# Moving the decay frame to the chunk's end, with eps in spare columns and a re-searched order, in a one-core RWKV-6 and feed-forward kernel

## The chip, the cores and the metric

One core of one Trainium2 chip. The metric is the device time of one launch in microseconds (us). The time before is the median of its launches. A launch over 1.5% above the fastest of the same kernel counts as slow, and ratios use the others, the fast ones, alone. In the profile PE is TensorE, PEld its weight loads, DVE VectorE, ACT ScalarE, POOL GpSimd, and SP the engine whose queue issues nearly all DMA.

## The reference, cut to what matters

```python
# attention: 4 batches x 8 heads, 768 steps, head size 48
for t in range(S):
    cur = einsum(u * k_t, v_t)                   # outer product per head
    y[:, :, t] = einsum(r_t, state + cur)
    state = w_t[..., None] * state + einsum(k_t, v_t)
# then, on 3072 rows of 384:
rms = sqrt(mean(x * x) + 1e-06);  xn = x / rms * rms_g
out = (silu(xn @ w_gate) * (xn @ w_val)) @ w_out  # 384 -> 1536 -> 384
```

## The kernel before

The sequence is cut into six chunks of 128 steps; each chunk has four batches. Within a chunk the recurrence is matmuls: `lw` is the logarithm of `w`, a matmul with a triangular mask sums it along the chunk, and its exponential scales r and k (`rkA`). A transposed copy (`rkT`) gives the products q, the mask cuts them, and q times v plus r times the state gives y. The state is carried from chunk to chunk. When a chunk's y is done, its rows are normalised (`xnr`), transposed (`xnt`) and go through the feed-forward part, while the next chunk's attention runs. A chunk change is the time at which PE goes over to the next chunk's log sums.

Everything is emitted in the order of one long string of steps; each engine executes its own steps in that order. `ld` is a load, `cs` the log sums, `rk` the scaling, `st` the state's matmuls, `sn` its update, `xn` the normalising, `xd` a transpose by DMA, `vc` a cast of v, `gv` a gate or value matmul, `warm` a matmul without use that keeps TensorE's clock up.

```python
def st_mm(self, m, j):                       # chunk m, batch j
    if m:                                    # old state enters PSUM by an identity matmul
        self.nc.tensor.matmul(ps, lhsT=self.ident, rhs=self.st[:, m % 2, j]..., start=True, stop=False)
    for i in range(NP):
        self.nc.tensor.matmul(ps[:, ...], lhsT=self.pair(ka, i), rhs=self.pair(v, i), ...)

def st_new(self, m, j, half):                # twice per batch: the two diagonal halves, decayed
    self.nc.vector.tensor_tensor(out=new[p, :, c], in0=ps[p, :, c], in1=wc[p, :]..., op=ALU.mult)

def x_rstd(self, m, j):
    self.nc.gpsimd.tensor_scalar(out=t[:, 0:1], ..., scalar1=1.0 / DM, scalar2=1e-6, op0=ALU.mult, op1=ALU.add)
    self.nc.gpsimd.tensor_tensor(out=t[:, 1:2], in0=t[:, 0:1], in1=self.mhalf, op=ALU.pow)

def xn_mul(self, m, j):                      # all 24 on DVE
    self.nc.vector.tensor_scalar(out=self.xnr[...], in0=self.xb[...], scalar1=self.rstd[...], op0=ALU.mult)
# ... (cut)
```

## Time and profile before

| | before |
|---|---|
| time, median (range) | 224.79 us (224.17 to 226.67), 3 launches |
| profiled span | 224.1 us |
| PE's dense start | 32.1 us |
| waits of PE after it | 9.2 us in twelve gaps |
| end of PE, then tail | 220.6 us, 3.5 us |

A busy share says little here, since PE's 91% holds warming matmuls and matmuls at half clock. What counts is where PE stands still and what released it. The lines for this are in the prediction.

### The profile page before, as it was taken

How to read it: one execution, taken by the hardware profiler on the slowest of the kernel's cores; microseconds unless marked ns; L12 is line 12 of the kernel's file. 1: busy time of each engine (PE TensorE's matmuls, PEld its weight loads, DVE VectorE, ACT ScalarE, POOL GpSimd, SP SyncE). 2: the span in 40 equal slices, each digit the busy share in tenths (PEclk: the TensorE clock that was granted, in tenths of full speed). 3: DMA queues.
4: the chain of work that ended last, by engine and by line, in shares of the span. 5: the costliest groups of instructions: out<-in, count | busy, mean ns of one | idle time of the engine just before them, and what ended most of it. 6: DMA issues, size and time to landing. Idle time of an engine off the chain costs nothing.

```text
span 224.1 us, 4873 instructions
## 1 busy us (share of the span) xinstructions
PE 204.1 (91%) x1844; PEld 125.7 (56%) x1844; DVE 162.8 (73%) x277; ACT 123.4 (55%) x221; POOL 97.6 (44%) x142
## 2 busy tenths in 40 slices
PE   7879679999959999996798999899999999999993
PEld 2345459986637856873344556346454654444561
DVE  4089897573987899993787977999996997116420
ACT  2423895784673688477534478336787354155201
POOL 2177886153368787221582258926672130000000
PEclk9999988999967999999699999999999999999999
DMA  6899999993999889968899994999839321001023
GB/s 155 169 216 234 272 341 321 310 207 78 237 196 219 168 166 155 215 137 160 195 209 143 194 222 110 213 226 195 172 76 229 63 73 35 0 35 38 1 93 117
DMA packets 133848, 36.95 MB, mean 165 GB/s; under 512 B 124481, under 2 KB 133825, under 8 KB 133825
## 3 DMA queue, kind: packets, MB, share of 16 engines
q1 hardware_dynamic: 133824, 36.65, 75.2%
q8 instruction: 14, 0.23, 0.4%
q14 instruction: 10, 0.07, 0.1%
HBM read 26.15 MB, written 4.72 MB: 138 GB/s over the span
## 4 chain that ended last, share of the span: by engine, by line
PE 53%; DVE 18%; DMA 11%; ACT 5%; issue 5%; SPq 5%; POOL 1%; DVEq 0%; ACTq 0%; POOLq 0%
PE ps L504 28%; PE ps L520 14%; DMA rkT<-rkA 6%; DVE rkA L375 4%; SPq L290 4%; PE ps L491 3%; DVE qts L403 3%; DVE st L434 3%; DVE ht L512 3%; DMA in_rk<-in_r_dram 2%; ACT junk L464 2%; DVE xb L460 2%; PE ps L400 2%; DMA in_w<-in_w_dram 2%; DMA in_rk<-in_k_dram 2%
## 5 line engine op out<-in xcount | busy, mean ns | idle before, releaser
L508 ACT ACTIVATE sg<-ps 128x512 bf16<-128x512 f32 x72 | 42.5, 595 | 45.9 <-PE ps L504 33.8
L512 DVE TENSOR_TENSOR ht<-ps,sg 128x512 bf16<-128x512 f32 x72 | 48.0, 684 | 22.8 <-ACT sg L508 15.7
L504 PE MATMUL ps<-xnt,wv 128*128 128x128 bf16 (+2 forms) x360 | 57.3, 301 | 0.5 <-DVE ht L512 0.5
L504 PE MATMUL ps<-xnt,wg 128*128 128x128 bf16 (+2 forms) x360 | 56.8, 299 | 0.6 <-DVE xnt L342 0.6
L520 PE MATMUL ps<-wo,ht 128*128 128x384 bf16 x288 | 51.5, 326 | 0.0
L504 PEld LDWEIGHTS <-wg 128*128 128x128 bf16 x360 | 29.4, 100 | 17.4 <-issue 1.7
L504 PEld LDWEIGHTS <-wv 128*128 128x128 bf16 x360 | 29.4, 101 | 16.5 <-issue 1.0
L520 PEld LDWEIGHTS <-ht 128*128 128x128 bf16 x288 | 27.6, 98 | 19.5 <-DVE ht L512 0.9
L456 POOL TENSOR_TENSOR ydr<-in_v,diag 128x384 f32<-128x384 f32 x24 | 20.6, 864 | 23.1 <-DVE diag L451 14.1
L403 DVE TENSOR_TENSOR qts<-ps,mask_lt 128x1024 bf16<-128x1024 f32 x24 | 28.8, 1216 | 1.4 <-PE ps L400 1.3
L444 POOL TENSOR_TENSOR ruk<-in_rk 128x384 f32<-128x384 f32 x24 | 24.2, 1010 | 9.9 <-DMA in_rk<-in_r_dram 4.8
L375 DVE TENSOR_TENSOR rkA<-in_rk,ps 128x768 bf16<-128x768 f32 x24 | 22.3, 947 | 4.8 <-ACT ps L372 2.8
L448 POOL TENSOR_TENSOR ruk<-ruk,u_bc 128x384 f32<-128x384 f32 x24 | 23.9, 998 | 1.6
L372 ACT ACTIVATE ps<-ps 128x768 f32<-128x768 f32 x24 | 18.8, 798 | 10.1 <-PE ps L367 9.2
L469 POOL TENSOR_SCALAR rstd<-rstd 128x1 f32<-128x1 f32 x24 | 5.2, 216 | 35.6 <-ACT junk L464 34.9
L464 ACT ACTIVATE junk<-xb 128x384 bf16<-128x384 bf16 x24 | 12.5, 520 | 13.0 <-DVE xb L460 12.9
L491 PE MATMUL ps<-mask_lt 128*128 128x512 bf16 x60 | 16.4, 415 | 1.3 <-POOL mask_lt L255 1.3
L333 ACT ACT_TABLE_LOAD x12 | 15.4, 1283 | 0.9 <-PEq L564 0.7
L434 DVE TENSOR_TENSOR st<-ps,wcr 48x192 bf16<-48x192 f32 x40 | 13.4, 352 | 1.1 <-ACT wcr L360 0.4
L470 POOL TENSOR_TENSOR rstd<-rstd,mhalf 128x1 f32<-128x1 f32 x24 | 13.3, 556 | 2.0
L451 DVE TENSOR_REDUCE diag<-ruk 128x8 f32<-128x384 f32 x24 | 12.9, 544 | 1.5 <-POOL ruk L448 1.4
L460 DVE TENSOR_TENSOR xb<-ps,ydr 128x384 bf16<-128x384 f32 x24 | 12.8, 548 | 1.3 <-PE ps L416 1.1
(62 smaller groups left out, 197.4 us busy)
## 6 DMA issues: line engine op xcount, KB each, us to landing
in_rk<-in_k_dram SPq DMA_DIRECT2D x24, 192.0 KB, 3.8
in_w<-in_w_dram SPq DMA_DIRECT2D x24, 192.0 KB, 3.9
in_rk<-in_r_dram SPq DMA_DIRECT2D x24, 192.0 KB, 3.8
in_v<-in_v_dram SPq DMA_DIRECT2D x24, 192.0 KB, 3.9
out_dram<-obr SPq DMA_DIRECT2D x24, 192.0 KB, 2.1
ht<-in_moe_w_gate_dram SPq DMA_DIRECT2D x4, 384.0 KB, 4.9
ht<-in_moe_w_val_dram SPq DMA_DIRECT2D x4, 384.0 KB, 6.1
ht<-in_moe_w_out_dram SPq DMA_DIRECT2D x4, 384.0 KB, 5.5
```

The source lines that it names most:

```text
L372: self.nc.scalar.activation(out=ps, in_=ps, func=AF.Exp)
L375: self.nc.vector.tensor_tensor(out=self.rkA[:, self.slot["rkA", m, j], :, :, 0:D], in0=self.in_rk[:, self.slot["in_rk", m], j], in1=self.b ...
L403: self.nc.vector.tensor_tensor(out=self.qts[:, self.slot["qts", m, j]].rearrange("p a q t -> p (a q) t"), in0=self.b2(("qb", m, j)).rearra ...
L434: self.nc.vector.tensor_tensor(out=new[p, :, c], in0=ps[p, :, c], in1=wc[p, :].to_broadcast([D, NP, D]), op=ALU.mult)
L444: self.nc.gpsimd.tensor_tensor(out=self.ruk[:, self.slot["ruk", m, j]], in0=rk[:, 0], in1=rk[:, 1], op=ALU.mult)
L448: self.nc.gpsimd.tensor_tensor(out=t, in0=t, in1=self.u_bc, op=ALU.mult)
L456: self.nc.gpsimd.tensor_tensor(out=self.ydr[:, self.slot["ydr", m, j]], in0=self.in_v[:, self.slot["in_v", m], j], in1=self.diag[:, m * SB ...
L491: self.nc.tensor.matmul(self.b1(("warmb",)), lhsT=self.mask_lt, rhs=bc_mid(self.mask_lt, 4), start=True, stop=True)
L504: self.nc.tensor.matmul(ps[:, a * n:(a + 1) * n], lhsT=w[:, c, f * 128:(f + 1) * 128], rhs=x[:, c], start=(a == 0 and c == 0), stop=(a == ...
L508: self.nc.scalar.activation(out=self.sg[:, self.slot["sg", m, g, i]], in_=self.b1(("gvb", m, g, i, "g")), func=AF.Silu)
L512: self.nc.vector.tensor_tensor(out=self.ht[:, self.slot["ht", m], fs[0]:fs[-1] + 1, t0:t0 + n], in0=self.b1(("gvb", m, g, i, "v")).rearran ...
L520: self.nc.tensor.matmul(ps, lhsT=self.ht[:, self.slot["ht", m], f, j * L:(j + 1) * L], rhs=self.wo[:, f, :], start=(f == 0), stop=(f == FC ...
```

## The change

It has five parts. (1) The frame of the decay moves to the chunk's end: the old state is decayed first (on POOL in 17 of 20 cases), used, and added to the new products on DVE, so the identity matmul goes. (2) The 1e-6 sits in four spare columns of `xb`, so that the sum of squares contains it and one POOL operation per row block goes. (3) Normalising and copies are spread over DVE, ACT and POOL. (4) The first chunk's feed-forward runs on groups of two batches; weights come in rows of 3 KB, and there are 36 warming matmuls instead of 60. (5) The order of all steps was searched again.

```diff
-        if m:
-            self.nc.tensor.matmul(ps, lhsT=self.ident, rhs=self.st[:, m % 2, j]..., start=True, stop=False)
-    def st_new(self, m, j, half):
-        self.nc.vector.tensor_tensor(out=new[p, :, c], in0=ps[p, :, c], in1=wc[p, :]..., op=ALU.mult)
+    def st_add(self, m, j, eng="DVE"):
+        if m:
+            self.nc.vector.tensor_tensor(out=self.sf[:, j], in0=ps, in1=self.st[:, m % 2, j], op=ALU.add)
+        else:
+            self.copy(eng, self.sf[:, j], ps)
+    def st_decay(self, m, j, eng):
+        (self.nc.vector if eng == "DVE" else self.nc.gpsimd).tensor_tensor(
+            out=self.st[:, m % 2, j]..., in0=self.sf[:, j]..., in1=self.wcr[...].to_broadcast([128, NP, 2, D]), op=ALU.mult)
-        for i, mask in ((0, self.mask_lt), (1, self.mask_nle)):
+        for i, mask in ((0, self.mask_nge), (1, self.mask_gt)):
# ... (cut)
+        for i, c in enumerate(EPS):              # EPS = four numbers, their squares / 384 sum to 1e-6
+            nc.vector.memset(self.xb[:, :, DM + i], c)
-        self.nc.gpsimd.tensor_scalar(out=t[:, 0:1], ..., scalar1=1.0 / DM, scalar2=1e-6, op0=ALU.mult, op1=ALU.add)
-    def xn_mul(self, m, j):
-        self.nc.vector.tensor_scalar(...)
+    def xn_mul(self, m, j, eng):
+        self.scale(eng, out, x, self.rstd[:, m * SB + j, 1:2])
-GROUPS = {0: ((0, 1), (1, 1), (2, 1), (3, 1)),
+GROUPS = {0: ((0, 2), (2, 2)), ...
# ... (cut: the order, and loads and casts of the weights)
```

## The prediction

> **What bounds the kernel now.** I read the page's shares first, then busy time by stage, then the gaps on TensorE (PE), then the groups.
>
> ```profile
> PE 204.1 (91%) x1844; PEld 125.7 (56%) x1844; DVE 162.8 (73%) x277; ACT 123.4 (55%) x221; POOL 97.6 (44%) x142
> PEclk9999988999967999999699999999999999999999
> DMA  6899999993999889968899994999839321001023
> ```
>
> PE is busy 91%, but that counts matmuls that only keep it warm and busy time at half clock, so the page alone doesn't settle it. The table by stage does (columns: stretch, its length, then busy time and count of PE, PEld, DVE, ACT, POOL, then granted clock, DMA share, GB/s):
>
> ```profile
> 20.00:32.00 12.00, 8.25 (x118) 5.64 (x115) 11.00 (x26) 9.70 (x23) 9.14 (x14) 1.00 0.99 267
> 32.00:49.00 17.00, 16.88 (x277) 16.81 (x277) 11.63 (x24) 12.22 (x28) 8.40 (x13) 0.90 1.05 295
> 80.00:97.00 17.00, 16.31 (x196) 12.29 (x195) 16.63 (x29) 11.39 (x20) 8.71 (x14) 1.00 0.95 178
> 97.00:110.00 13.00, 9.66 (x96) 6.22 (x95) 9.49 (x18) 9.76 (x15) 4.34 (x7) 0.90 0.71 153
> 150.00:165.00 15.00, 14.49 (x127) 8.14 (x126) 14.66 (x28) 10.56 (x18) 10.41 (x15) 1.00 0.88 180
> 181.00:200.00 19.00, 19.00 (x106) 9.32 (x105) 8.57 (x17) 8.02 (x17) 2.25 (x6) 1.00 0.14 37
> ```
>
> There are three regimes. Up to 32 us DMA is full and PE waits for inputs or runs warming matmuls. From 32 us PE carries the time, with DVE beside it at 98% where two chunks of attention overlap (80 to 97 and 150 to 165 us). From 181 us PE alone is full. So I cut the span at PE's dense start:
>
> ```profile
> 32.12 1.34 PE L504 MATMUL ps<-xnt,wg 128*128 128x128 bf16 x12 [0.60 <-DVE xnt L342]
> 64.66 0.50 PE L480 MATMUL ps<-ident,xnr 128*128 128x128 bf16 x3 [1.35 <-DVE xnr L473]
> 107.31 0.47 PE L367 MATMUL ps<-lw,mask_nle 128*128 128x384 bf16 x1 [2.96 <-DVE obr L342]
> 208.88 11.71 PE ps L520 x72
> ```
>
> The first three are from PE's timeline, with the gap before each in brackets. The last is the end of the chain of waits: 72 output matmuls in one piece to 220.6 us. Twelve bracketed gaps lie after 32.1 us (0.3, 0.8, 1.4, 0.4, 0.2, 0.5, 3.0, 0.4, 0.7, 0.6, 0.5, 0.5), 9.2 us together. Half clock after gaps costs more: in 5 us stretches the granted clock is 0.93 at 35 us, 0.52 at 65, 0.74 at 105 (half of it idle) and 0.92 at 110, so 0.35 + 2.4 + 0.7 + 0.4, plus 0.65 for the first 12 feed-forward matmuls, which took 1.34 us instead of 0.67: 4.5 us. So the span of 224.1 us is 32.1 us until the dense start, then 188.5 us to PE's end (9.2 of gaps, 4.5 of slow clock, about 174.8 of work), and 3.5 us of tail.
>
> **What the Trainium skill says.** "TensorE: Matmul & The Clock Gate", section "Wait — 56ns, not 53.3ns?", gives the warm start-to-start time as N/2.4 GHz plus about 2.5 ns. The trace agrees: 72 output matmuls of 384 columns in 11.71 us are 162.6 ns each, and 168 of 128 columns in 9.38 us (chain, at 39.6 us) are 55.8 ns. The same page, "What's actually happening", says that the clock falls to half after at least one idle window of some 3.4 us and comes back after a busy one. The clock of 0.52 after the gaps around 62 to 66 us fits. "SBUF — State Buffer", section "SBUF: two separate sides", says that POOL and some DVE operations take a shared port pair as an exclusive lock. The normalising multiply on DVE has a median of 311 ns and a longest of 1043 ns, which fits such blocking but doesn't prove it. "DMA: Bandwidth & Descriptors", "Why small descriptors are slow (HBM only)", puts a fixed cost on each packet. Here stretches of nothing but 192-byte rows moved about 215 GB/s at full DMA share, and stretches with weights in 1 KB rows up to 340.
>
> **The change, part by part.**
>
> *Identity matmul.* Sixteen matmuls of 384 columns (chunks 1 to 4, four batches) go: in the timeline such a one is followed by the next matmul after 0.17 us. 16 x 0.165 = 2.6 us less on PE, all after 32 us, so all of it counts.
>
> *State update.* Before, 40 DVE multiplies of 352 ns, 13.4 us. After, 16 DVE adds of PSUM and old state plus two copies on DVE and two on ACT. The nearest row is the addition into xb (PSUM plus SBUF, 384 columns, 548 ns): 18 x 0.55 = 9.9 us. The decay is 17 times on POOL, nearest row ydr<-in_v,diag with 864 ns: 14.7 us, and three times on DVE, 1.7 us. DVE's saving is only 13.4 - 11.6 = 1.8 us. The decay now needs this chunk's log sums, but its reader also waits for exponentials, a DMA transpose (3.2 us to landing) and the mask, so a decay of 0.9 us has slack.
>
> *Eps in spare columns.* 24 POOL operations go: 5.2 us of POOL, and some 0.2 us from each chain square, power, multiply, transpose. The square has 388 columns instead of 384: nothing.
>
> *Placement.* Of 24 normalising multiplies (458 ns) DVE keeps 13, minus 5.0 us; ACT takes 7 (about 0.5 us as its other 384-column work), POOL 4 (1.3 us, an estimate from 937 ns for 256 columns and some 0.2 us fixed). Transposed copies move from DVE (6 to 1, minus 3.4 us at 682 ns) to ACT (2 to 7, plus 5.1 us). Sums: DVE 162.8 - 1.8 - 5.0 - 3.4 and about -0.5 of small items = 152; ACT 123.4 + 3.5 + 5.1 - 2 (fewer casts, more copies) = 130; POOL 97.6 + 14.7 + 5.2 - 5.2 + 0.7 = 113. None becomes a bound over the whole; DVE is relieved by perhaps 2 us in each of its full stretches.
>
> *Chunk 0's feed-forward* goes from 288 matmuls of 128 columns to 144 of 256: 288 x 55.8 = 16.1 us against 144 x 110 = 15.8. Nothing in stream time; half the weight loads, in the stretch where PEld is 99% busy. But weights are now cut by contraction rows, so the first block needs three pieces per matrix instead of one.
>
> *Start.* Before the first block can run densely, the new order has loaded sixteen inputs of 0.197 MB, u, and seven weight pieces of 0.393 MB. At the rates above: 3.35 MB / 215 GB/s = 15.6 us, 2.75 MB / 335 GB/s = 8.2 us, plus 2.7 us to the first landing and some 1.5 us for a queue that isn't full at first: 28 us. Cast, value matmul and transposes add 1.5 to 2: dense start at about 30 us against 32.1. Gain 2 us. Warming matmuls fall from 60 to 36, which is worth nothing by itself: they fill waits.
>
> *Order.* The largest gap (3.0 us at 104) comes from DVE, which sat 3.3 us before a value cast until 105.08 us because the loads stood behind two DMA transposes in the issue queue; PE then lacked a bank. In the new order chunk 3's value loads stand before the second transpose of that group. Also fewer transposed copies and multiplies queue on DVE at 60 to 66 us. I take half of the 9.2 us of gaps as gone (4.6), and of the slow clock nearly half (2).
>
> *Sum:* 2.6 + 0.3 + 2 + 4.6 + 2 = 11.5 us at best guess; I give back 2.5 us for new waits that a searched order gets wrong on the chip. Net 9: span 215, and as the timed median is 0.7 us above the span, 216 us.
>
> **Rivals.**
> (a) *Only the matmul.* The gaps move, total unchanged: 224.8 - 2.6 - 0.3 = 222. For it: gaps come from in-order queues meeting DMA landings, which a search doesn't know exactly. Against: the largest is a named ordering fault, and the change to placement unloads the DVE where it is full.
> (b) *The start gets worse.* DMA is full until 50 us and the first block waits for six pieces instead of two. If casts or slot waits hold the issue queue, the dense start slides to 34 us or more, with warming inside: 222 to 226. For it: the new order itself keeps some warming matmuls between chunk 0's feed-forward blocks. Against: weight rows are three times longer (3 KB), and the scale column is issued early on another queue, where before it landed at 10.2 us.
> (c) *POOL becomes the new wait.* 14.7 us of decay on POOL stand before the power operation that every normalised row needs, and the shared lock lengthens DVE. Then PE waits for transposed rows: 221 to 226. For it: the 1043 ns case. Against: POOL has 10 to 15 us free in most chunks, and loses 24 small operations.
> (d) *Nearly all gaps close.* 224.8 - 2.9 - 3 - 9.2 - 4.5 = 205; I think 208 the practical limit, as some waits at chunk changes are in the data flow.
>
> **Range and chances.** The sum centres on 216; (d) bounds it below, (a) above. Eight in ten: 209 to 222. Faster by over 2% means below 220.3, which needs half of the expected saving: 0.77. Within 2%: 0.20. Slower: 0.03, since nothing adds work to PE.
>
> **What would show it.** The rows: no identity matmul, 16 DVE adds near 550 ns, decays on POOL near 0.86 us, no second POOL operation before the power. PE's timeline: dense feed-forward from about 30 us, gaps after that of 5 us or less in sum, no gap of 3 us at the change to chunk 3. The stage table: DVE below 95% where it was 98%, POOL near 113 us in all. Wrong if the dense start is later than 32 us, if PE's gaps after it still sum to 9 us, if the low-clock stretches are as many as before, or if POOL's decay or power operation is named as the releaser of long waits.

## The result, and the profile after

The changed kernel took 217.87 us (217.25 to 218.17, 4 launches) against 224.64 us (4 launches, one more than in the table above); the ratio is 0.9701, with a 95% interval of 0.9648 to 0.9754: faster. Here and below, a ratio is the mean time of one kernel's fast runs over that of the other's of the same rounds, so not quite the ratio of the medians quoted.

Three lines of the page after:

```profile
PE 194.1 (90%) x1660; PEld 119.0 (55%) x1660; DVE 151.8 (70%) x244; ACT 128.1 (59%) x232; POOL 111.4 (52%) x139
PEclk9999999999999999999699999999999999999999
DMA  6999979999999899999999798999557512221013
```

PE's busy time is 10 us less, of which 24 fewer warming matmuls are a part that buys nothing. DVE, ACT and POOL are near what the sums foretold (152, 130 and 113). The clock falls in one slice instead of several; read in shorter stretches it is at half from about 103.6 to 107 us. And the DMA row holds 7 or more, after its first slice, for 27 of the 40 slices; before, slices of 3, 6 and 4 lay among them.

The new rows, one line for each form (busy us, mean ns of one, then idle before it and its releaser):

```profile
L441 DVE TENSOR_TENSOR sf<-ps,st 128x384 f32<-128x384 f32 x16 | 8.6, 546 | 1.7 <-PE ps L435 1.7
L446 POOL TENSOR_TENSOR st<-sf,wcr 128x384 bf16<-128x384 f32 x17 | 14.0, 828 | 2.3 <-ACT wcr L363 2.2
L446 DVE TENSOR_TENSOR st<-sf,wcr 128x384 bf16<-128x384 f32 x3 | 2.2, 721 | 0.0
L477 POOL TENSOR_TENSOR rstd<-rstd,mhalf 128x1 f32<-128x1 f32 x24 | 13.5, 565 | 26.9 <-ACT junk L472 26.8
L345 POOL TENSOR_SCALAR xnr<-xb,rstd 128x384 bf16<-128x384 bf16 x4 | 5.0, 1251 | 0.3
L343 ACT ACTIVATE xnr<-xb,rstd 128x384 bf16<-128x384 bf16 x7 | 4.2, 607 | 0.8 <-POOL rstd L477 0.8
L345 DVE TENSOR_SCALAR xnr<-xb,rstd 128x384 bf16<-128x384 bf16 x13 | 6.4, 502 | 1.6 <-POOL rstd L477 1.6
```

The add on DVE takes 546 ns (0.55 us was predicted), the decay on POOL 828 (864), the multiply on POOL 1251 (1300). No second POOL operation stands before the power.

PE's timeline, the lines with its longest waits (wait and releaser in brackets), and the end of the chain of waits:

```profile
32.91 0.81 PE L511 MATMUL ps<-xnt,wg 128*128 128x256 bf16 x6 [0.52 <-DVE xnt L335]
59.49 0.40 PE L411 MATMUL ps<-rkT 48*128 48x128 bf16 x8 [0.77 <-ACT rkT L339]
92.58 0.40 PE L411 MATMUL ps<-rkT 48*128 48x128 bf16 x8 [1.14 <-DVE ht L519]
101.81 0.32 PE L370 MATMUL ps<-lw,mask_nge 128*128 128x384 bf16 x1 [1.72 <-DVE rkA L386]
131.19 0.32 PE L370 MATMUL ps<-lw,mask_nge 128*128 128x384 bf16 x1 [0.40 <-DVE rkA L386]
```
```profile
206.60 5.87 PE ps L527 x36
```

Ten gaps after the dense start sum to 5.4 us (0.77, 0.17, 0.16, 0.24, 1.14, 1.72, 0.21, 0.33, 0.40, 0.23). The dense start itself is at 32.9 us, later than before. Cut as in the prediction:

| us | before | after | difference |
|---|---|---|---|
| until the dense start | 32.1 | 32.9 | +0.8 |
| PE's waits after it | 9.2 | 5.4 | -3.8 |
| half clock | 5.8 | 1.7 | -4.1 |
| work at full clock (the rest) | 173.5 | 172.5 | -1.0 |
| tail after PE's end (212.5) | 3.5 | 3.8 | +0.3 |
| span | 224.1 | 216.3 | -7.8 |

The half clock is worked out from stretches of 0.25 us, as PE's busy time there times what the granted clock lacks to 1. The prediction's 4.5 us for before is too small. It came from stretches of 5 us, whose mean clock also counts time in which PE stands idle. Before, the clock was down from 32.2 to 35.7, 63.0 to 69.8 and 107.3 to 110.7 us, which cost 1.7, 2.6 and 1.5 us. The work after holds five warming matmuls behind the dense start, some 1.1 us.

One more view was not in the prediction's argument, though its columns were on the table: both kernels in the two stretches from 50 to 150 us (length; busy us and count of PE, PEld, DVE, ACT, POOL; granted clock, DMA share, GB/s). Before, then after:

```profile
50.00:100.00 50.00, 46.43 (x511) 34.19 (x510) 42.75 (x74) 32.51 (x60) 27.78 (x39) 0.93 0.88 175
100.00:150.00 50.00, 44.83 (x354) 23.32 (x351) 39.93 (x64) 27.36 (x44) 25.20 (x33) 0.97 0.96 182
```
```profile
50.00:100.00 50.00, 47.27 (x552) 35.53 (x551) 44.98 (x68) 38.95 (x71) 39.20 (x45) 1.00 1.03 195
100.00:150.00 50.00, 47.08 (x380) 24.74 (x379) 42.24 (x62) 28.62 (x50) 28.16 (x35) 0.97 0.99 191
```

PE is at 94%, and DMA at 99 to 103% (a share over 1 shows that this measure is no strict ceiling). In these 100 us DMA moves 193 GB/s instead of 178.5 (the means of the two stretches). So the middle of the kernel may have two near-bounds, and the new order also keeps the second one fuller.

### The profile page after: what moved, and what is told of

Read it like the earlier page. It is cut to its first block, busy times and chain, and to the rows that moved or that the text cites.

```text
span 216.3 us, 4472 instructions
## 1 busy us (share of the span) xinstructions
PE 194.1 (90%) x1660; PEld 119.0 (55%) x1660; DVE 151.8 (70%) x244; ACT 128.1 (59%) x232; POOL 111.4 (52%) x139
## 4 chain that ended last, share of the span: by engine, by line
PE 67%; SPq 8%; POOL 8%; DMA 5%; issue 4%; ACT 4%; DVE 2%; ACTq 0%; POOLq 0%; DVEq 0%
PE ps L511 37%; PE ps L527 16%; SPq L290 7%; PE ps L498 4%; PE ps L411 2%; PE ps L370 2%; DMA rkT<-rkA 2%; PE ps L427 2%; DMA xnt<-xnr 2%; POOL st L446 1%; POOL ydr L464 1%; PE ps L399 1%; POOL ruk L452 1%; DVE rkA L386 1%; PE ps L424 1%
## 5 line engine op out<-in xcount | busy, mean ns | idle before, releaser
L515 ACT ACTIVATE sg<-ps 128x512 bf16<-128x512 f32 x72 | 41.4, 596 | 37.4 <-PE ps L511 30.3
L511 PE MATMUL ps<-xnt,wg 128*128 128x256 bf16 (+1 forms) x288 | 56.3, 330 | 0.9 <-DVE xnt L335 0.5
L511 PE MATMUL ps<-xnt,wv 128*128 128x256 bf16 (+1 forms) x288 | 55.7, 329 | 0.0
L527 PE MATMUL ps<-wo,ht 128*128 128x384 bf16 x288 | 53.5, 326 | 0.0
L511 PEld LDWEIGHTS <-wv 128*128 128x128 bf16 x288 | 27.9, 99 | 18.2 <-issue 1.4
L511 PEld LDWEIGHTS <-wg 128*128 128x128 bf16 x288 | 27.1, 98 | 17.2 <-issue 1.9
L472 ACT ACTIVATE junk<-xb 128x388 bf16<-128x388 bf16 x24 | 12.6, 524 | 12.9 <-DVE xb L468 12.8
L370 PE MATMUL ps<-lw,mask_nge 128*128 128x384 bf16 x24 | 8.5, 354 | 11.3 <-ACT lw L329 8.4
L446 POOL TENSOR_TENSOR st<-sf,wcr 128x384 bf16<-128x384 f32 x17 | 14.0, 828 | 2.3 <-ACT wcr L363 2.2
L339 ACT COPY obr<-ps 128x384 f32<-128x384 f32 x14 | 6.6, 478 | 12.6 <-PE ps L527 12.4
```

What stands on the lines that cost most here:

```text
L446: (self.nc.vector if eng == "DVE" else self.nc.gpsimd).tensor_tensor(out=self.st[:, m % 2, j].rearrange("p q (a d) -> p q a d", a=2), in0= ...
L511: self.nc.tensor.matmul(ps[:, a * n:(a + 1) * n], lhsT=w[:, c, f * 128:(f + 1) * 128], rhs=x[:, c], start=(a == 0 and c == 0), stop=(a == ...
L515: self.nc.scalar.activation(out=self.sg[:, self.slot["sg", m, g, i]], in_=self.b1(("gvb", m, g, i, "g")), func=AF.Silu)
L527: self.nc.tensor.matmul(ps, lhsT=self.ht[:, self.slot["ht", m], f, j * L:(j + 1) * L], rhs=self.wo[:, f, :], start=(f == 0), stop=(f == FC ...
```

## The experiments

Twelve runs on four chips. The kernel before took 225.35, 225.74, 225.71 and 226.06 us on them. A run is read by its ratio to the kernel before of its own rounds; ratios with intervals of about 0.005 to each side tell a step of 1% apart, not one of 0.3%.

Theory: PE is the bound after its dense start, so each us taken from PE's stream or from the chains that feed it counts. Rival: in the middle PE only runs up to the next chunk change, where the feeding queues let it go; a us saved on PE is then waited away. The first batch undoes one part at a time.

### The changed kernel again, as the yardstick

> The changed kernel once more, as the level that the other runs of this batch are read against. Expected at the same ratio to the kernel before as on record, 0.970 within 0.4%.

217.37 us (216.44 to 219.69), ratio 0.9647 (0.9593 to 0.9701). The profile had PE's dense start at 32.63 us and its gap at the change to chunk 3 at 101.28 us, of 1.79 us.

### The identity matmul back

```diff
+        if m:   # result overwritten by the next matmul: same values, no new wait
+            self.nc.tensor.matmul(ps, lhsT=self.ident, rhs=v.rearrange("p h d -> p (h d)"), start=True, stop=True)
```

> The changed kernel with sixteen identity matmuls of 384 columns put back on TensorE, ahead of the state's own matmuls, their result overwritten (no new wait, result still right). My theory, TensorE's stream is the bound from 33 us on: 16 x 0.165 = 2.6 us longer than the changed kernel, ratio to before about 0.982. Rival, they fall into gaps that exist anyway (5.4 us of them): under 1 us longer, ratio 0.974 or less.

218.82 us (217.73 to 219.48), ratio 0.9708 (0.9660 to 0.9757): 1.45 us more than the yardstick for 2.6 us of stream, and not clearly apart from it. The gap at the change to chunk 3 fell from 1.79 to 0.77 us, but this doesn't show added work lying in a wait that was there anyway: the gap ended 0.96 us earlier (100.32 against 101.28 us), since DVE's multiply and cast in front of it ran faster. DVE of the yardstick, then of this run:

```profile
97.82 0.88 DVE L345 TENSOR_SCALAR xnr<-xb,rstd 128x384 bf16<-128x384 bf16 x1 [0.31 <-POOL rstd L477]
98.62 1.75 DVE L335 CAST vb<-in_v 128x1536 bf16<-128x1536 f32 x1
```
```profile
97.58 0.32 DVE L345 TENSOR_SCALAR xnr<-xb,rstd 128x384 bf16<-128x384 bf16 x1
97.95 1.45 DVE L335 CAST vb<-in_v 128x1536 bf16<-128x1536 f32 x1
```

In sum PE's waits after the start fell only from 5.2 to 4.7 us. And the clock did not fall in this run (0.999 or 1.000 in all six launches), where its fall takes about 1.6 us of PE's time in the yardstick's profile. So where the other 1.15 us went stays open; the rival's mechanism is one candidate.

### The second POOL operation back

```diff
+        self.nc.gpsimd.tensor_scalar(out=t[:, 0:1], in0=t[:, 0:1], scalar1=1.0 / DM, scalar2=1e-6, op0=ALU.mult, op1=ALU.add)
```

> The changed kernel with eps added again by an operation on GpSimd (24 more operations of about 0.2 us, the square on 384 columns). My theory: 5 us more of GpSimd, off the path but for the chain at the change to chunk 3, so 0 to 0.5 us longer. Rival: the trace shows GpSimd on the chain of waits from 79 to 99 us, so the eight operations there add up to 1.5 us or more.

219.51 us (217.90 to 220.06), ratio 0.9735 (0.9680 to 0.9790): 2.1 us more, where I expected half a us at most (the intervals of the two ratios overlap a little; both ran in the same rounds). POOL is busy 5 us more (116.1), PE has the same work. PE's timeline of this run at the change to chunk 3:

```profile
103.86 0.48 PE L370 MATMUL ps<-lw,mask_nge 128*128 128x384 bf16 x1 [2.86 <-DVE rkA L386]
```

The gap grew by 1.07 us. On DVE, the last normalising multiply before it had to wait 1.10 us for POOL's power instead of 0.31. The rest came in small pieces, 0.6 us of it before the dense start. An operation of 0.2 us costs little busy time, but it stands before each of the 24 power operations, and at this change DVE's multiply, and PE behind it, wait for that chain.

### The new state operations in the old order

The kernel before with `sf`, the zero-blocked decay, the add and the POOL decay, but with its own frame, order and placements.

```diff
-        if m:
-            self.nc.tensor.matmul(ps, lhsT=self.ident, rhs=self.st[...], start=True, stop=False)
-        self.st_new(m, j, 0)                                              # step sn1
+        self.nc.vector.tensor_tensor(out=self.sf[:, j], in0=ps, in1=self.st[:, m % 2, j], op=ALU.add)
-        self.st_new(m, j, 1)                                              # step sn
+        self.nc.gpsimd.tensor_tensor(out=self.st[:, (m + 1) % 2, j]..., in0=self.sf[:, j]..., in1=self.wcr[...], op=ALU.mult)
```

> The kernel before in its old order and frame, but with the new state operations: no identity matmul, old state added on VectorE, decay on GpSimd. My theory: the 2.6 us of TensorE come off, with little lost to a GpSimd queue whose order was not searched for this: 1.5 to 2.6 us faster than before, ratio 0.988 to 0.994. Rival, the new operations pay only with a new order: no gain or slower, ratio 0.998 or more.

226.55 us (226.05 to 228.32), ratio 1.0068 (1.0014 to 1.0123): a little slower than before, although PE's stream is shorter. PE's timeline:

```profile
65.00 0.50 PE L487 MATMUL ps<-ident,xnr 128*128 128x128 bf16 x3 [1.62 <-DVE xnr L480]
107.33 0.32 PE L370 MATMUL ps<-lw,mask_nle 128*128 128x384 bf16 x1 [2.11 <-DVE obr L343]
```

The waits of before at 65 and 107 us (1.35 and 2.96 there) are still there, and PE's waits after the start sum to 11.5 us instead of 9.2; the largest new one, 1.63 us at 34.7, is for a weight cast on POOL. POOL rises to 112.3 us, and its decay has 3% of the chain that ended last. So in the old order the new state operations, taken together, pay nothing; what the removed matmul alone would pay there isn't shown. (The frame was not changed here: the decay still follows the add, so it isn't the change's state update in every respect.)

### All decays on DVE

```diff
-... dm.1.0/G ... dm.1.1/G ...        # and 15 more
+... dm.1.0/V ... dm.1.1/V ...
```

> The changed kernel with all twenty decays on VectorE instead of three. Seventeen more of some 0.72 us are 12 us of VectorE, 14 us less of GpSimd. Theory that VectorE is the partner bound where two chunks overlap: 2 to 4 us longer than the changed kernel. Rival, GpSimd is the wait at the change to chunk 3 (it is on the chain there for 20 us): 0 to 1 us faster.

220.42 us (219.61 to 223.53), ratio 0.9732 (0.9677 to 0.9786). The medians differ by 3 us, but the yardstick ran on another chip; by the ratios it is 0.9%, some 1.9 us more, just under the 2 to 4 expected, and the intervals overlap. DVE rises to 161.0 us, and the gap at the change to chunk 3 to 2.71 us. So in this order POOL is the better place for the decay, by an amount that isn't settled; the fear that it would delay the power operation is outweighed by what DVE loses.

### The named ordering fault, mended in the kernel before

The prediction put the gap of 3.0 us at 107 us down to two loads of v that stood behind two DMA transposes in the issue queue. Here they stand ahead of them.

```diff
-... ld.3.2.v ... xd.2.1@0 ... xd.2.2 ... ld.3.3.v ... ld.3.0.v
+... ld.3.2.v ld.3.3.v ld.3.0.v ... xd.2.1@0 ... xd.2.2 ...
```

> The kernel before with one edit: two value loads of chunk 3 are issued ahead of the DMA transposes instead of behind two of them. If the gap of 3 us on TensorE at 104 us came from that order, it closes, and with it the low clock after it: 2 to 3.5 us faster than before, ratio 0.985 to 0.991. If another wait (the transposed rows of the next block) stands right behind it: under 1 us, ratio 0.996 or more.

226.90 us (224.04 to 227.90, 22 launches), ratio 1.0022 (0.9996 to 1.0049): no gain. PE's timeline:

```profile
105.30 0.32 PE L367 MATMUL ps<-lw,mask_nle 128*128 128x384 bf16 x1 [0.68 <-DVE obr L342]
...
113.41 0.40 PE L400 MATMUL ps<-rkT 48*128 48x128 bf16 x8 [1.30 <-DVE rkA L375]
...
138.82 0.32 PE L367 MATMUL ps<-lw,mask_lt 128*128 128x384 bf16 x1 [1.51 <-DVE rkA L375]
```

The cause was named correctly: the gap shrank from 2.96 to 0.68 us. But waits opened behind it, and all waits after the start sum to 10.5 us instead of 9.2. That something else came late because these loads went first is likely, but wasn't traced.

### The late warming matmuls away

In the changed kernel, the dense start is at 32.9 us although the inputs that I had tallied for 28 us had landed by about 28.9 (ACT's cast of batch 3's v waited for its load until 28.86). PE's timeline after:

```profile
28.52 0.33 PE L487 MATMUL ps<-ident,xnr 128*128 128x128 bf16 x3
...
30.98 1.24 PE L498 MATMUL ps<-mask_lt 128*128 128x512 bf16 x5
32.06 0.33 PE L487 MATMUL ps<-ident,xnr 128*128 128x128 bf16 x3
```

The first transpose runs at 28.5 us; its partner, ready as early, stands in PE's order behind attention of other batches and thirteen warming matmuls, and runs at 32.06. ACT also had five weight casts in a row until 31.9 us.

```diff
-warm.25 ... warm.26 warm.27 ... warm.35
```

> The changed kernel without its last eleven warming matmuls (six before the first feed-forward block, five between the first blocks). If they only fill waits: no change, within 0.5 us. If TensorE would have had work ready: up to 11 x 0.216 = 2.4 us faster; the first block waits for a weight cast that ends at 31.9 us where it began at 32.9, so my number is 1 to 2 us faster than the changed kernel.

217.43 us (215.57 to 219.06), ratio 0.9614 (0.9559 to 0.9668): within noise of the yardstick. PE was dense at 30.75 us and 1.3 us ahead at 58 us (57.90 against 59.22 for the same matmuls). Then, on PE and on DVE:

```profile
100.56 0.32 PE L370 MATMUL ps<-lw,mask_nge 128*128 128x384 bf16 x1 [2.62 <-DVE rkA L386]
```
```profile
98.68 0.96 DVE L335 CAST vb<-in_v 128x1536 bf16<-128x1536 f32 x1 [1.62 <-DMA in_v<-in_v_dram]
99.56 2.68 DVE L386 TENSOR_TENSOR rkA<-in_rk,ps 128x768 bf16<-128x768 f32 x3
```

PE came early and waited 0.8 us longer than in the yardstick, because DVE's cast waited for a load of v. At the next change nothing was left of the lead (130.89 against 130.95 us). This is the rival, seen directly: the lead is given back at chunk changes.

### The first feed-forward block moved ahead as well

```diff
-... xt.0.1@3 ... xe.0.1/V ... ldwo.0@2 gv.0.0.2.g@4        # after y.0.3, st.0.3, xa.0.2, xa.0.3
+... wc.4.g.1/A warm.21 xt.0.1@3 ... xe.0.1/V ... gv.0.0.2.g@2 gv.0.0.2.v@0 y.0.3@6 ...
```

> The same without the eleven, and the first feed-forward block moved ahead: its last weight cast before the casts of the second half of the weights, the transposes and copies of its rows before the mask of batch 3, its matmuls before the last value matmuls of chunk 0. Theory that the dense start was late through order and not through DMA: it begins at about 30 us instead of 32.9, 2 to 2.9 us faster than the changed kernel (ratio about 0.958). If DMA set it: no faster than the run without the eleven.

218.31 us (216.45 to 220.23), ratio 0.9632 (0.9573 to 0.9691). The start came at 30.64 us in the profile, and nothing clear of it stayed in the time. The profiled launch was slow, so its gaps aren't compared. Two tries at an earlier start, no gain from either.

### Fewer bytes in the middle (a wrong result on purpose)

```diff
+        n = H // 2 if m in (2, 3, 4) and w != "w" else H    # half the heads of r, k, v
```

> The changed kernel, with only half of the heads of r, k and v loaded in chunks 2, 3 and 4 (wrong result on purpose: the other half keeps older data), 36 transfers of 0.1 MB instead of 0.2. New theory, the transfers are a second bound from 50 to 150 us and make the gaps at the changes to chunks 3 and 4: those two close, 3 to 5 us faster than the changed kernel. Rival, the gaps come from VectorE's and GpSimd's queues: under 1 us.

214.84 us (214.14 to 215.92), ratio 0.9517 (0.9474 to 0.9561): some 1.3% or 2.9 us faster than the yardstick. The DMA share from 50 to 100 us fell to 0.76. PE's gaps at 92 and 131 us vanished, that at 100.37 us stayed, with 2.07 us. So in part both are true: the loads pace some changes, while the gap at the change to chunk 3 doesn't go away with their bytes.

### More bytes in the middle

```diff
+        for _ in range(2 if m in (3, 4) and w == "v" else 1):   # the same load twice
```

> The changed kernel, with the eight value loads of chunks 3 and 4 issued twice (same data, right result): 8 x 0.95 = 7.6 us more of the DMA engines, at an estimate. New theory, DMA a full second bound: 4 to 8 us longer than the changed kernel. Rival, TensorE alone is the bound and DMA has room: under 1.5 us.

238.65 us (237.82 to 239.65), ratio 1.0560: 21 us more, far outside both theories. The experiment measured something else. The waits of the issue queue, from 60 to 170 us:

```profile
SPq L291 <- DMA in_v<-in_v_dram: 20.7, 8, 3.7
```

Each second load writes what the first one writes, so its issue waited until the first had landed: eight times, 20.7 us in all, while everything behind it in that queue stood still. The DMA share from 100 to 150 us fell from 0.99 to 0.76. It doesn't weigh bytes. That the standstill and the added time are nearly equal is one case and no rule: in the yardstick the same queue stands still for 7.8 us at one point of the same stretch (for a multiply on DVE), and no gap of PE there is over 1.8 us.

### Loads in the order of need

On the kernel without late warming, two loads of r of the next chunk change places with loads needed sooner.

```diff
-... ld.4.0.r@0 ... ld.3.2.v ... ld.3.1.v          +... ld.3.1.v ... ld.3.2.v ... ld.4.0.r@0
-... ld.5.0.r@1 ... ld.4.1.r                       +... ld.4.1.r ... ld.5.0.r
```

> The changed kernel without its eleven late warming matmuls, and two pairs of loads swapped, so that a load of chunk 3 goes ahead of one of chunk 4, and one of chunk 4 ahead of one of chunk 5. If the gaps at the changes (2.6 and 1.5 us in the run without the eleven) come from loads standing in the wrong order in a full queue: both shrink to under 1 us and the time falls by 2 to 3 us against that run. If the queue is full whatever its order, something else comes late: under 1 us.

216.84 us (215.83 to 218.34), ratio 0.9615 (0.9573 to 0.9658): no gain over the run without late warming. The gap at 131 us closed, and DVE's cast no longer waited for its load. The gap at the change to chunk 3 stayed. On PE and on DVE:

```profile
101.68 0.32 PE L370 MATMUL ps<-lw,mask_nge 128*128 128x384 bf16 x1 [2.08 <-DVE rkA L386]
```
```profile
98.22 0.88 DVE L345 TENSOR_SCALAR xnr<-xb,rstd 128x384 bf16<-128x384 bf16 x1 [0.31 <-POOL rstd L477]
99.02 1.75 DVE L335 CAST vb<-in_v 128x1536 bf16<-128x1536 f32 x1
100.69 2.67 DVE L386 TENSOR_TENSOR rkA<-in_rk,ps 128x768 bf16<-128x768 f32 x3
```

DVE is busy without a break, and the scaling that frees PE's bank stands behind a cast of 1.75 us that PE doesn't need yet. ACT then idled 1.98 us.

### That cast on ACT

```diff
-... dm.3.1/G vc.3.0.4@1/V xd.2.1 ... rk.3.1@0 exp.3.2 ld.3.3.r
+... dm.3.1/G xd.2.1 ... rk.3.1@0 exp.3.2 vc.3.0.4@1/A ld.3.3.r
```

> Base: the changed kernel without late warming matmuls and with chunk 4's r loads behind chunk 3's v loads (216.84 us, ratio 0.9615). Only edit: chunk 3's value cast (128 x 1536) goes from DVE, where it stood for 1.75 us between the last normalising multiply and the three rk multiplies, to ACT, behind the third exponential, where ACT then idled 1.98 us. Theory (the gap of 2.08 us at 101.7 us is DVE's queue): the rk multiplies come 1.3 to 1.7 us earlier, PE's gap there falls to 0.9 us or less and, as no loads wait at the next change, 0.8 to 1.5 us of it stay in the time: about 215.7 us, ratio 0.956 to 0.958. Rival (the changes are paced by the chain of loads and transposes, and what closes here opens behind it): the gap shrinks, but other gaps at 131 to 140 us grow by as much; ratio 0.960 to 0.963. Third: the cast on ACT delays the next exponential or the state matmuls, and the gap stays near 2 us.

215.87 us (215.53 to 216.48), ratio 0.9572 (0.9528 to 0.9616), as expected. On PE and on DVE:

```profile
98.48 0.32 PE L370 MATMUL ps<-lw,mask_nge 128*128 128x384 bf16 x1 [0.41 <-DVE rkA L386]
...
100.18 0.50 PE L435 MATMUL ps<-vb,rkA 128*128 128x96 bf16 x8 [1.22 <-ACT obr L339]
```
```profile
96.69 0.88 DVE L345 TENSOR_SCALAR xnr<-xb,rstd 128x384 bf16<-128x384 bf16 x1 [0.32 <-POOL rstd L477]
97.49 2.71 DVE L386 TENSOR_TENSOR rkA<-in_rk,ps 128x768 bf16<-128x768 f32 x3
```

The scaling follows the multiply at once, and the gap falls to 0.41 us. The state's matmuls then wait 1.22 us for ACT, so part of the wait only moved (my third possibility, in part). In the two profiles PE's waits after the start don't fall in sum (5.4 us in the run it builds on, 5.8 here): waits of 0.4 to 0.7 us stand at 107, 108, 114 and 138 us, much as the rival said. What else differs is a start 1.8 us earlier, though emitted alike, and the clock, which no longer falls (a loss of 1.7 us in the run before, by the working above). This is the fastest kernel with a right result, 0.8% under the yardstick by the ratios. It isn't clearly apart from the run that it builds on (0.9615), but all of its six launches lie under 216.5, and of the changed kernel's ten only one does. That it beats both kernels is likely; that the mended wait is what did it isn't shown.

## Why the prediction was right or wrong

**Right: the total, and the direction of all terms but one.** 216 us against 217.87, inside 209 to 222. The engine sums, the rows and the removed POOL operation came out as worked out. PE's gaps fell by 3.8 us (4.6 was taken), the half clock by 4.1 (2 was taken), the work by 1.0 (2.9 was taken; the five warming matmuls behind the start explain some 1.1 of the rest). Of the profile's signs, gaps "of 5 us or less in sum" (5.4) and "no gap of 3 us at the change to chunk 3" (1.72) hold or nearly so. DVE's two full stretches eased, in the same windows, from 98 to 94% (16.01 of 17 us) and to 79% (11.79 of 15).

**Wrong: the start.** "dense start at about 30 us" was derived from what must be loaded. The loads took nearly what they were said to take (28.9 us against 28), but PE began its dense work 4.0 us later, where 1.5 to 2 were allowed. In the trace, PE's own order, warming matmuls and the row of casts on ACT stand between. The prediction had set this as a mark of being wrong: "later than 32 us". The step that failed is taking the last landing as the start without reading the order of PE and ACT behind it. And its worth was also wrong: with the start at 30.75 us, nothing clear stayed. A caution belongs to this: three runs whose start is emitted alike had it at 30.75, 33.75 and 31.98 us, so one profile doesn't settle 2 us there, and how much of the delay the warming matmuls make isn't settled either.

**Wrong: the worth of single parts.** "so all of it counts", said of the identity matmul's 2.6 us, met 1.45. "some 0.2 us from each chain" for the eps operation, to which the sum gave nothing, met 2.1 us. The "named ordering fault" really was a fault, and mending it alone gave nothing. The errors have, as I read them, one source: the sum added savings on PE as if PE alone set the pace. At a chunk change PE waits for a chain over ACT, POOL and DVE. What shortens that chain can count; what shortens PE before it can be waited away. The run with the second POOL operation back shows the first, the run without the late warming matmuls the second; for the identity matmul it is a guess. POOL's share of the chain that ended last rose from 1 to 8%, so rival (c) was partly at work too.

**Luck in the total.** Start (2.8 us), work (1.9), gaps (0.8) and tail (0.3) fell short of the sum by 5.8 us. The clock gave 2.1 us more than was taken, and 2.5 us had been held back for another reason, for new waits. So the span came out 1.2 us off because errors of both signs nearly cancelled.

**The clock.** Its rise is measured; its worth is not. Five of the changed kernel's ten launches had a granted clock of 1.00 and averaged 217.65 us; the four fast ones at 0.99 averaged 217.46. One half-clock window between two chunk changes leaves no mark in the time, which fits the same explanation. The prediction's reading that the clock of 0.52 "fits" the gaps at 62 to 66 us is loose: it fell at about 63.0 us, before the largest of them.

**Not settled.** How the 6.8 us divide between frame, placement and order isn't shown: undone singly, the identity matmul, eps and the decay's place make 1.45, 2.1 and some 1.9 us, but they aren't independent, and the state operations alone made the old order slower. The search's order as a whole was not tried without them. That fuller DMA in the middle is itself a cause of the gain is argued from the table and from the run with fewer bytes, not shown by a run of its own.

## What to carry to other kernels

Before a saving is counted at full value, ask which queue lets the bounding engine go at the next stage change: here 24 operations of a fifth of a microsecond in that chain were worth 2.1 us, and 2.6 us of the busy engine's own work 1.45. When one wait is mended, look at the next stage change for where it went, and judge by the time, not by the gap. And when an engine stands busy in front of the instruction that others wait for, try moving what nobody waits for yet to an engine that idles then, and look at what stands behind it there.

## What the Trainium skill lacked or had wrong

- "GPSIMD Engine Reference", section "4.1 Engine selection", has POOL about two times slower than DVE for operations with two inputs and near line rate for one. Here it is the other way round: the decay, with two input tensors, took 828 ns on POOL and 721 on DVE (647 in the run with all twenty there), while the normalising multiply, with one tensor of 384 columns, took 1251 ns on POOL and on DVE had a mean of 502 and a median of 320. The measurement decides: of the two, the decay is what POOL does nearly as well.
- "DMA: Bandwidth & Descriptors", section "Two DMAs through the same engine are not ordered", says to make the issuing engine wait for the first transfer before a dependent one is issued, but not what that costs on a queue that carries everything: here eight such waits held it for 20.7 us, and the kernel took 21 us longer.
- "TensorE: Matmul & The Clock Gate", section "What's actually happening", ties the fall to half clock to an idle window of some 3.4 us. The window need not be empty: in the changed kernel the clock fell at about 103.6 us, and the 3.4 us before it held 1.25 us of PE work, with no single gap over 1.72 us. In the kernel before it fell at about 63.0 us, with 2.27 us of PE work in the 3.4 us before and no gap over 0.81. A stage change that is only thin in PE work can be enough. The page's section "A second HAM failure mode: psum-queue depth-cycling" has a case of short idles that let the clock swing, but doesn't say how little work is enough.
